# Two groups of block sums on GpSimd instead of VectorE, and another bank for the last token pair's chain

## The chip, the cores and the metric

The kernel runs on one core of one Trainium2 chip. Its time is the device time of one execution in microseconds (us). An execution that was recorded by the hardware profiler has a time of its own, and inside it the span from the first to the last instruction. The engines are TensorE (PE), VectorE (DVE), ScalarE (ACT), GpSimd (POOL) and SyncE (SP, which here only issues DMAs). Each engine works through its own instructions in order; semaphores order the engines against each other.

## The reference

2048 tokens of 512 numbers are normalised (layer norm without weights). The result is the input plus two branches of the normalised tokens `xn`:

```python
qkv = xn @ wqkv                                # 32 heads of 16
logits over the 8 positions s, s-2, ..., s-14  # masked below 0
A = softmax(logits) weighted v, then @ wo
topk_idx = argsort(-(xn @ w_gate))[:, :2]      # 2 of 8 experts
B = sum over the two experts e of gate * (silu(xn @ w1[e]) @ w2[e])   # 512 -> 1792 -> 512
out = x + A + B
```

## The kernel before

**Arithmetic.** Every operand of a matrix product is split into a high and a low part in 16 bits; a product is three passes of PE (high*high, low*high, high*low). `xnT` holds the normalised tokens, transposed, as those two parts.

**Stages on PE, in order.** First the column groups 0 and 1 of `wqkv` for 16 tiles of 128 tokens (`q_pass`, L365 to L383, with the gate's columns in group 0). Then groups 2 and 3 for eight pairs of token tiles (`product`, L481 to L492): a Strassen-like scheme with seven products for each pair `p_`, named m1 to m7, 56 in all. Then 112 blocks of the experts' first product (`up`, L912 to L925) alternating with the second (`down`, L945 to L973), and at the end the product with `wo` (`o_mm`, L1087). The attention itself is computed on DVE beside the experts.

**The sums that the seven products need.** For each group `b` of four token tiles, so for the pairs `2b` and `2b+1`, these steps run before the products m5, m6, m3 and m7 of those pairs:

- `fj_b` (`f_join`, L436): high plus low part of `xnT`, 128x2048, into a 32-bit tile `f`. Groups 0 and 1 (b < NF) use one tile of the pool `fre`; groups 2 and 3 use one of the pool `atp`, which can be opened once `fre` is closed (the task `swapR`).
- `fs_b` (`s_sums`, L444): four sums or differences of 128x512 in that tile.
- `sh_b_0`, `sh_b_1` (`s_hi`, L457): ScalarE copies of 128x1024 to 16 bits, the high part.
- `sl_b_0`, `sl_b_1` (`s_lo`, L462): 128x1024 subtractions, the low part.

All but `sh` are instructions of DVE with two inputs in SBUF.

**The chain of one pair.** The products accumulate in three PSUM banks: a (m1, m6, m7, m4), c (m2) and d (m5, m3). Between the products of bank a ScalarE reads the partial sum out (x11, x12, xu, x21) and between those of d as well (x22); DVE adds parts together (y22, L499; y11 and y12, L507). Bank a is one of two buffers with the tag "up", which the experts' first product uses later. Each pair ends with a store (`pst`).

**Routing.** When the gate's logits of all tokens stand in `glog`, DVE ranks the tokens (`r_top`, L533 to L566: 13 instructions with two SBUF inputs and some with one), PE counts them (`r_count`, L568), DVE goes on (`r_rank`, `r_hot0` to `r_hot2`), PE makes the lists (`r_list1`, `r_list2`, L644), and DVE writes them out (`r_lis`, L647). From then on POOL gathers tokens by indirect DMA (`ga`, L851), SP transposes them (`tx`, L858), and the first block of the experts (`up0`) can start.

**The order.** The order of the instructions on every engine is fixed before the kernel is built, by a planner written out in the file (`Plan.solve`, L72). Each task has an engine, a planned duration, and tasks it depends on (`deps`: their end; `begun`: their begin). PE's tasks have a priority by hand (`prio`), from which their due times follow; from these each other task gets a latest start (`late`), lowered by `HURRY` for `r_lis` and so for what it depends on. Then a list scheduler plays the program through: on each engine the ready task of lowest rank comes next (rank: `prio` on PE, `late` elsewhere). `r_count` and `r_list` have the priority -1000 on PE: they take the next place once they are ready in the plan. The planned durations are `d2(n)` for DVE and `act(n)` for ScalarE, both of n elements in a partition; what engines do to each other's speed is not in it. The order that comes out is final: PE doesn't pass by a task whose input is late.

```python
r = max(r, end[d] + (0.0 if tk[d][0] == t[0] and not tk[d][5] else LAT.get(tk[d][0], 0.08)))
...
c = min((p, r, n) for r, p, n in lst if r <= t0)
```

Of the kernel before, what the change touches and what calls it, by code (L numbers as in the profile page):

```python
# [1 line left out]

# [18 lines left out]
KB = D // P  # L21
# [33 lines left out]

NS = NJ // 2
NP0 = 0
HURRY = dict(r_lis=20.0)
NF = 2
LAT = dict(PE=0.28, ACT=0.16, DVE=0.16, POOL=0.16)  # L60


class Plan:
    def __init__(self):
        self.tasks = {}

    def add(self, name, eng, dur, fn, deps=(), prio=0.0, svc=0.0, early=0.0, begun=(), lead=None, post=0.6):
        assert name not in self.tasks, name
        self.tasks[name] = (eng, dur, fn, [d for d in deps if d is not None], prio, svc, early,
                            [d for d in begun if d is not None], lead, post)  # L70

    def solve(self, start):  # L72
        tk = self.tasks
# [70 lines left out]
                if not left[o]:  # L144
                    release(o)
        assert len(order) == len(tk), [n for n in tk if n not in begin][:20]
        self.begin, self.end, self.order, self.late = begin, end, order, late

    def emit(self, names):
        for n in names:  # L150
# [6 lines left out]

def act(n):
    return 0.18 + n * 0.00087


def mm(*cols):
# [4 lines left out]
def layer_kernel(ctx: ExitStack, tc, x, wqkv, wo, wg, w1, w2, out):  # L167
# [265 lines left out]

    FT, SS = {}, {}

    def f_join(b):  # L436
        f = FT[b] = (fre if b < NF else atp).tile([P, 2048], F32, name=f"f_{b}", tag="f" if b < NF else "og", bufs=1)
        c_ = slice(512 * b, 512 * b + 512)
        v.tensor_tensor(f.rearrange("p (k c) -> p k c", k=KB), xnT[:, 0:KB, c_], xnT[:, KB:2 * KB, c_], op=ALU.add)

    def f_part(b, kh, e_):
        return FT[b].rearrange("p (h k q e t) -> p h k q e t", h=2, k=2, q=2, e=2)[:, kh, :, :, e_, :]

    def s_sums(b):  # L444
        f11, f12, f21, f22 = (f_part(b, kh, e_) for e_ in range(2) for kh in range(2))
        v.tensor_tensor(f22, f21, f22, op=ALU.add)
        v.tensor_tensor(f21, f11, f21, op=ALU.subtract)
        v.tensor_tensor(f11, f22, f11, op=ALU.subtract)
        v.tensor_tensor(f12, f12, f11, op=ALU.subtract)

    def s_dst(b, lo):
        return SS[b][:, lo].rearrange("p (h k m t) -> p k h m t", h=2, k=2, m=4)
# [7 lines left out]
        nc.scalar.copy(s_dst(b, 0)[:, kb], s_src(b)[:, kb])  # L460

    def s_lo(b, kb):  # L462
        v.tensor_tensor(s_dst(b, 1)[:, kb], s_src(b)[:, kb], s_dst(b, 0)[:, kb], op=ALU.subtract)

    s_at = dict(s1=(1, 1), s2=(0, 0), s3=(0, 1), s4=(1, 0))

# [14 lines left out]
    def product(p_, m):  # L481
        bank, l_, r_ = prods[m]
        if (p_, bank) not in MB:
            pp, tg = {"a": (pu, "up"), "c": (py, ("y0", "y2")[p_ % 2]), "d": (py, ("y1", "yt1")[p_ % 2])}[bank]
            MB[p_, bank] = pp.tile([P, 512], F32, name=f"pm_{p_}_{bank}", tag=tg)
        ps = MB[p_, bank][:, 0:384].rearrange("p (c t d) -> p c t d", c=2, t=3)
        t = unit[r_].rearrange("p a (k t c d) -> p a k c t d", k=2, t=3, c=2)
        first, last = m in ("m1", "m2", "m5"), m in ("m2", "m3", "m4")
        for i, (a, b) in enumerate(((0, 0), (1, 0), (0, 1))):
            for k in range(2):  # L490
                nc.tensor.matmul(ps, left_of(p_, l_, a, k), t[:, b, k], start=first and i == 0 and k == 0,  # L491
                                 stop=i == 2 and k == 1, skip_group_check=True)  # L492

    outs_of = dict(x11=("a", 0, 0), y11=("c", 0, 0), x12=("a", 1, 0), x22=("d", 1, 1), xu=("a", 0, 1), x21=("a", 0, 1), y12=("d", 1, 0))

    def take(p_, n):
        if n == "y22":
            e21, e22 = (pair_tile(p_)[:, 2 * cg:2 * cg + 2, :, 1, :] for cg in range(2))
            v.tensor_tensor(e22, e22, e21, op=ALU.add)  # L499
            return  # L500
        bank, cg, e_ = outs_of[n]
        dst = pair_tile(p_)[:, 2 * cg:2 * cg + 2, :, e_, :].rearrange("p c t d -> p (c t) d")
        src = MB[p_, bank][:, 0:384].rearrange("p (n d) -> p n d", d=H2)
        if n[0] == "x":
            nc.scalar.activation(dst, src, AF.Copy, scale=-1.0 / (SW * SX))
        else:
            v.scalar_tensor_tensor(dst, src, -1.0 / (SW * SX), dst, op0=ALU.mult, op1=ALU.add)  # L507
# [669 lines left out]
        add(f"uh_{n}", "ACT", act(768), B(u_hi, n), deps=([n] if n[0] == "t" else after[n]) + old)  # L1177
        add(f"ul_{n}", "DVE", d2(768), B(u_lo, n), deps=[f"uh_{n}"])
    for b in range(NP0 // 2, 4):
        add(f"fj_{b}", "DVE", d2(2048), B(f_join, b), deps=[f"tn_{j}" for j in range(4 * b, 4 * b + 4)] + ([f"sl_{b - 1}_1"] if NP0 // 2 < b != NF else []) + ["swapR"] * (b >= NF))  # L1180
        add(f"fs_{b}", "DVE", 4 * d2(512), B(s_sums, b), deps=[f"fj_{b}"])
        for kb in range(2):
            add(f"sh_{b}_{kb}", "ACT", act(1024), B(s_hi, b, kb), deps=[f"fs_{b}"] + ([f"{m}_{p_}" for p_ in (0, 1) for m in ("m3", "m5", "m6", "m7")] if b == 3 and kb == 0 else []),
                begun=[f"sh_{b}_0" if kb else f"sh_{b - 1}_1" if b > NP0 // 2 else None])
            add(f"sl_{b}_{kb}", "DVE", d2(1024), B(s_lo, b, kb), deps=[f"sh_{b}_{kb}"] + ([f"sl_{b}_0"] if kb else []))
    add("gate", "POOL", 0.6, gate_part, deps=["lgate"], prio=-39.5)
    for i, (cg, j) in enumerate(seq):
        n = 400 if cg == 0 else 384
# [54 lines left out]
    for p_ in range(NP0, NS):  # L1243
        b = p_ // 2
        own = lambda n: f"{n}_{p_}"
        free = {"a": [f"x21_{p_ - 2}"], "c": [f"y11_{p_ - 2}"], "d": [f"y12_{p_ - 2}"]} if p_ > NP0 + 1 else \
            dict(a=ev_of(ups[p_ - NP0 - 2]), c=last_of[(2, 4)[p_ % 2]], d=last_of[(3, 5)[p_ % 2]])
        after = dict(m1=[], m2=[], m6=["x11"], m7=["x12"], m5=[], m4=["xu"], m3=["x22"])
        for i, (m, (bank, l_, r_)) in enumerate(prods.items()):
            ready = [f"sl_{b}_{kb}" for kb in range(2)] if l_[0] == "s" else []  # L1250
            add(own(m), "PE", mm(*[384] * 6), B(product, p_, m), deps=[f"ul_{r_}"] + ready + [own(n) for n in after[m]] +
                (free[bank] if m in ("m1", "m2", "m5") else []), prio=10.0 * len(seq) + 5.0 * (7 * (p_ - NP0) + i))
        keep = [stores[len(order_g) + p_ - 3]]
        for n, m, more in (("x11", "m1", []), ("x22", "m5", []), ("x12", "m6", []), ("y12", "m3", ["x12"]), ("xu", "m7", []),
                           ("y22", "m7", ["xu", "x22"]), ("y11", "m2", ["x11"]), ("x21", "m4", ["y22"])):
            add(own(n), "ACT" if n[0] == "x" else "DVE", act(384) if n[0] == "x" else d2(384), B(take, p_, n),
                deps=[own(m)] + [own(x) for x in more] + keep)
        add(f"pst{p_}", "SP", 0.65, B(p_st, p_), deps=[own(n) for n in ("y11", "y22", "x21", "y12")], svc=2.4)


# [30 lines left out]
    for U in range(NP):  # L1291
# [4 lines left out]
        fr = [f"dn{2 * (U - 3) - 1}_3", f"up{2 * (U - 3) + 1}"] if U > 3 else ([f"up{2 * (U - 3) + 1}"] if U == 3 else [f"{m}_{2 * U + 2 + i}" for i in range(2) for m in ("m3", "m5", "m6", "m7")])  # L1296
        add(f"whi{U}", "ACT", act(n), B(w_hi, U, c_, unit_of(U), unit_of(U - 1)), deps=[f"ld{U}"] + fr, prio=G(2 * U - 3))
        add(f"wlo{U}", "DVE", d2(n), B(w_lo, U, c_), deps=[f"whi{U}"], prio=G(2 * U - 2.5))
    add("silu_t", "ACT", 1.5, lambda: nc.scalar.activation(root, eps, AF.Silu), deps=["x21_7"])
    add("swapL", "X", 0.0, swap_left, begun=stores + ["up0"])  # L1300
    for g, (e, f) in enumerate(blocks):
        U = g // 2
        cap = CAPS[e]
        cols = [cap] * 12 if cap <= 512 else [cap - 64] * 12 + [64] * 12
        bank = [f"si{g - 2}"] if g > 1 else [f"x21_{6 + g}"]
        if g == 0:
            bank += [f"tx0_{t}" for t in range(len(tiles_of(0)))]
        if f == 0 and e:
            bank += [f"tx{e}_{t}" for t in range(len(tiles_of(e)))]
        add(f"up{g}", "PE", mm(*cols), B(up, e, f), deps=bank + [f"wlo{U}"], prio=G(g))  # L1310
        sd = act(cap) + (0.25 if cap > 512 else 0.0)
        hb = [f"dn{g - LAG - 2}_3"] if g >= LAG + 2 else []
        add(f"si{g}", "ACT", sd, B(silu, e, f), deps=[f"up{g}", "swapL"] + ([f"hl{g - 3}"] if g > 2 else []), prio=G(g) - 3)
        add(f"hh{g}", "ACT", act(cap), B(h_hi, e, f), deps=[f"si{g}"] + hb, prio=G(g) - 3)
        add(f"hl{g}", "DVE", d2(cap), B(h_lo, e, f), deps=[f"hh{g}"], prio=G(g))
        t0 = NM if g == NG - 1 else 0
        for t in range(NM + 1):
            cols = [512] * 3 if t < NM else ([2 * (cap - CM)] * 4 + [cap - CM] * 4 if cap - CM <= P else [cap - CM] * 12)
            fr = []
            if f == 0 and e:  # L1320
                fr = [f"ye{e - 1}_{t}"] if t < NM else [f"yt{e - 1}_0", f"yt{e - 1}_1"]
            if g == 0:
                fr += ["y11_6", "y11_7", "y12_6", "y12_7"]
            add(f"dn{g}_{t}", "PE", mm(*cols), B(down, e, f, t), deps=[f"hl{g}", f"wlo{U + 1}"] + fr +
                ([f"dn{g}_{(t - 1) % 4}"] if t != t0 else []), prio=G(g + LAG) + 5 + 0.1 * ((t - t0) % 4))
    ys_use = []
# [223 lines left out]
```

## Time and profile before

| what | us |
|---|---|
| median of 3 runs | 760.68 (760.32 to 761.95) |
| the profiled execution | 759.91 |
| its span | 758.2 |
| PE busy, whole span | 751.8 |
| DVE busy | 665.3 |
| ACT busy | 399.8 |
| POOL busy | 110.1 |
| granted TensorE clock, mean | 1.000 |

"Busy" is the time in which an engine has an instruction under way; for PE the ends are modelled, since matmuls are pipelined. The rest of the page, and views of the same execution by stretches of time, are shown in the prediction where they are used. Positions in time are counted from the start of the span.

### The profile page before, as it was taken

What the parts mean: (1) busy time and instruction counts of PE and PEld (TensorE: products, weight loads), DVE (VectorE), ACT (ScalarE), POOL (GpSimd) and SP (SyncE); (2) the same over time, 40 slices, a digit from 0 to 9 for tenths busy, and PEclk for the clock granted to TensorE, in tenths of its full rate; (3) what the DMA queues carried; (4) which work ended last, traced back from release to release, by engine and by line L of the source; (5) the groups of instructions that cost most, each with busy time, mean ns of one, the idle gap of its engine ahead of it and who ended that gap; (6) DMA issues with size and microseconds to landing.
All of it is one profiled execution on the core that took longest, in us unless ns stands there. A gap on an engine that the chain in (4) does not pass through costs nothing.

```text
span 758.2 us, 12400 instructions
## 1 busy us (share of the span) xinstructions
PE 751.8 (99%) x4917; PEld 413.3 (55%) x4917; DVE 665.3 (88%) x632; ACT 399.8 (53%) x596; POOL 110.1 (15%) x107
## 2 busy tenths in 40 slices
PE   8999999999999999999999999999999999999997
PEld 4555665555555555555555555555555555555544
DVE  7897999999999899989989989999999899737355
ACT  6874356555457445753754574466447554754300
POOL 2010036040001300210030004002100000007171
PEclk9999999999999999999999999999999999999999
DMA  8999889685359647973693599358626943886476
GB/s 278 237 259 314 279 236 309 241 227 167 133 170 224 185 162 210 222 233 117 210 250 140 191 243 261 124 179 206 205 88 170 254 129 111 217 325 208 133 243 203
DMA packets 167377, 157.25 MB, mean 207 GB/s; under 512 B 81505, under 2 KB 135137, under 8 KB 167059
## 3 DMA queue, kind: packets, MB, share of 16 engines
q1 hardware_dynamic: 161571, 139.52, 62.9%
q0 software_dynamic: 5216, 16.88, 7.4%
q8 instruction: 39, 0.64, 0.4%
q14 instruction: 23, 0.19, 0.1%
q10 hardware_dynamic: 528, 0.02, 0.0%
HBM read 108.12 MB, written 29.56 MB: 182 GB/s over the span
## 4 chain that ended last, share of the span: by engine, by line
PE 97%; SPq 1%; DMA 1%; DVE 0%; issue 0%
PE pu L923 13%; PE pu L922 13%; PE pu L924 13%; PE y L955 10%; PE y L954 10%; PE y L953 10%; PE pw L1092 5%; PE pq L383 5%; PE pm_a L491 4%; PE yt L964 3%; PE pq L381 2%; PE pm_d L491 2%; PE yt L965 2%; PE yt L973 2%; PE yt L971 2%; PE yt L972 2%
## 5 line engine op out<-in xcount | busy, mean ns | idle before, releaser
L923 PE MATMUL pu<-xgt,w 128*128 128x64 f16 (+8 forms) x616 | 184.6, 321 | 0.0
L922 PE MATMUL pu<-xgt,w 128*128 128x64 f16 (+8 forms) x616 | 184.4, 321 | 0.0
L924 PE MATMUL pu<-xgt,w 128*128 128x64 f16 (+8 forms) x616 | 180.4, 321 | 0.0
L930 ACT ACTIVATE hs<-pu 128x64 f32<-128x64 f32 (+8 forms) x154 | 69.6, 481 | 186.3 <-PE pu L924 186.1
L897 DVE SCALAR_TENSOR_TENSOR w<-s,w 128x2048 f16<-128x2048 f32 (+1 forms) x57 | 128.2, 2249 | 18.6 <-ACT w L888 18.4
L888 ACT ACTIVATE w<-s 128x2048 f16<-128x2048 f32 (+1 forms) x57 | 107.3, 1883 | 59.2 <-PE yt L965 29.4
L955 PE MATMUL y<-w,hh 128*128 128x512 f16 x336 | 127.5, 379 | 0.0
L954 PE MATMUL y<-w,hh 128*128 128x512 f16 x336 | 127.5, 379 | 0.0
L953 PE MATMUL y<-w,hh 128*128 128x512 f16 x336 | 127.4, 379 | 0.0
L851 POOL DMA_INDIRECT xg<-xr,lis x35 | 64.9, 1854 | 419.1 <-DMA xgt<-xg 359.6
L940 DVE SCALAR_TENSOR_TENSOR hh<-hs,hh 128x550 f16<-128x550 f32 (+7 forms) x112 | 76.6, 687 | 26.2 <-ACT hh L936 26.1
L924 PEld LDWEIGHTS <-w 128*128 128x128 f16 x616 | 58.9, 97 | 48.5
L922 PEld LDWEIGHTS <-w 128*128 128x128 f16 x616 | 59.3, 97 | 41.0
L923 PEld LDWEIGHTS <-w 128*128 128x128 f16 x616 | 59.0, 97 | 40.9
L936 ACT ACTIVATE hh<-hs 128x550 f16<-128x550 f32 (+7 forms) x112 | 70.5, 631 | 3.4
L807 DVE TENSOR_TENSOR pv<-vt,at 128x4096 f32<-128x4096 f32 x16 | 70.7, 4422 | 0.3
L780 DVE TENSOR_TENSOR pq<-kt,qt 128x4096 f32<-128x4096 f32 x16 | 70.7, 4420 | 0.2
L784 DVE TENSOR_REDUCE at<-pq 128x256 f32<-128x4096 f32 x16 | 70.6, 4412 | 0.0
L1075 POOL DMA_INDIRECT yg<-yd,yrow x32 | 36.5, 1139 | 172.5 <-DVE hh L940 146.1
L813 DVE TENSOR_TENSOR pv<-pv 128x2048 f32<-128x2048 f32 (+1 forms) x32 | 56.1, 1753 | 0.2
L955 PEld LDWEIGHTS <-hh 128*128 128x128 f16 x336 | 32.8, 98 | 39.7
L953 PEld LDWEIGHTS <-hh 128*128 128x128 f16 x336 | 32.8, 98 | 34.2
(207 smaller groups left out, 1018.1 us busy)
## 6 DMA issues: line engine op xcount, KB each, us to landing
s<-in_B_w SPq DMA_DIRECT2D x112, 512.0 KB, 4.3
kt<-qd SPq DMA_DIRECT2D x8, 960.0 KB
vt<-qd SPq DMA_DIRECT2D x8, 960.0 KB, 6.5
qd<-qe SPq DMA_DIRECT2D x8, 768.0 KB, 4.5
qd<-qp SPq DMA_DIRECT2D x8, 768.0 KB, 6.7
yd<-ys SPq DMA_DIRECT2D x24, 256.0 KB, 3.1
xr<-xh SPq DMA_DIRECT2D x16, 256.0 KB, 4.2
qt<-qd SPq DMA_DIRECT2D x8, 512.0 KB, 7.0
```

Of the source, the lines that this page charges most:

```text
L780: v.tensor_tensor(A["pr"].rearrange("p (j w d) -> p j w d", w=WIN, d=H2), a_win(A["k", c], hf, False), qb.to_broadcast([P, 8, WIN, H2]), o ...
L784: v.tensor_reduce(A["at", c][:, 8 * hf:8 * hf + 8].rearrange("p j w h -> p (j w h)"), A["pr"].rearrange("p (n d) -> p n d", d=16), axis=AX ...
L807: v.tensor_tensor(A["pr"].rearrange("p (j w h d) -> p j w h d", w=WIN, h=NH, d=16), a_win(A["v", c], hf, True), ab.to_broadcast([P, 8, WIN ...
L888: nc.scalar.activation(w[:, 0, c_], stg[k][:, c_], AF.Copy, scale=SW)
L897: v.scalar_tensor_tensor(w[:, 1, c_], stg[k][:, c_], SW, w[:, 0, c_], op0=ALU.mult, op1=ALU.subtract)
L922: nc.tensor.matmul(ps, a_[:, 0, kb, fs], xh, start=kb == 0, stop=False)
L923: nc.tensor.matmul(ps, a_[:, 0, kb, fs], xl, start=False, stop=False)
L924: nc.tensor.matmul(ps, a_[:, 1, kb, fs], xh, start=False, stop=kb == KB - 1)
L940: v.scalar_tensor_tensor(hh[:, 1, c_], hsd[key, f][:, c_], SH, hh[:, 0, c_], op0=ALU.mult, op1=ALU.subtract)
L953: nc.tensor.matmul(y_, hi, b_[:, 0, :], start=st, stop=False)
L954: nc.tensor.matmul(y_, hi, b_[:, 1, :], start=False, stop=False)
L955: nc.tensor.matmul(y_, lo, b_[:, 0, :], start=False, stop=sp)
```

## The change

`PB = (1, 2)`: `fj`, `fs` and `sl` of the groups 1 and 2 become instructions of GpSimd, with a planned duration of their own, `gp(n)`. For the last pair (`p_ == NS - 1`, so 7) bank a is the bank "yt0" instead of an "up" buffer, free after `r_lis`; the partial result xu goes to the memory of the weight part b11 (`spare`), which m1_7 is the last to read, so that x21 need not wait for y22. `up0` and `up1` wait for the pairs 5 and 6 instead of 6 and 7; the load of ScalarE's table for the experts (`silu_t`) follows x12_7 instead of x21_7. `up0` begins after m4_7 and `up1` after `up0`, as a condition now; `hl0` and `hl1` follow y11_7, y22_7 and y12_7. `HURRY` for `r_lis` is 12 instead of 20. The planner's result is put in order once more, so that a task can be emitted behind others (`behind`) on each engine's unchanged order.

```diff
-HURRY = dict(r_lis=20.0)
+HURRY = dict(r_lis=12.0)
...
+PB = (1, 2)
...
-        self.begin, self.end, self.order, self.late = begin, end, order, late
+        self.begin, self.end, self.late = begin, end, late
...
+            for d in set(tk[n][3]) | set(tk[n][7]) | set(self.behind[n]) | ({prev[e]} if e in prev and e != "X" else set()):
...
+def gp(n):
+    return 0.25 + n * 0.0021
...
+    def s_eng(b):
+        return nc.gpsimd if b in PB else v
...
-        v.tensor_tensor(f.rearrange("p (k c) -> p k c", k=KB), xnT[:, 0:KB, c_], xnT[:, KB:2 * KB, c_], op=ALU.add)
+        s_eng(b).tensor_tensor(f.rearrange("p (k c) -> p k c", k=KB), xnT[:, 0:KB, c_], xnT[:, KB:2 * KB, c_], op=ALU.add)
...
-        v.tensor_tensor(f22, f21, f22, op=ALU.add)
+        s_eng(b).tensor_tensor(f22, f21, f22, op=ALU.add)
...
-        v.tensor_tensor(s_dst(b, 1)[:, kb], s_src(b)[:, kb], s_dst(b, 0)[:, kb], op=ALU.subtract)
+        s_eng(b).tensor_tensor(s_dst(b, 1)[:, kb], s_src(b)[:, kb], s_dst(b, 0)[:, kb], op=ALU.subtract)
...
-            pp, tg = {"a": (pu, "up"), "c": (py, ("y0", "y2")[p_ % 2]), "d": (py, ("y1", "yt1")[p_ % 2])}[bank]
+            pp, tg = {"a": (pu, "up") if p_ < NS - 1 else (py, "yt0"), "c": (py, ("y0", "y2")[p_ % 2]), "d": (py, ("y1", "yt1")[p_ % 2])}[bank]
...
+    def spare():
+        return unit["b11"].rearrange("p a c -> p (a c)").bitcast(F32)[:, 0:384].rearrange("p (n d) -> p n d", d=H2)
...
+            if p_ == NS - 1:
+                e21 = spare()
...
+        if n == "xu" and p_ == NS - 1:
+            dst = spare()
...
+        se, sd = ("POOL", gp) if b in PB else ("DVE", d2)
+        add(f"fj_{b}", se, sd(2048), B(f_join, b), deps=[f"tn_{j}" for j in range(4 * b, 4 * b + 4)] + ([f"sl_{b - 1}_1"] if NP0 // 2 < b != NF else []) + ["swapR"] * (b >= NF))
+        add(f"fs_{b}", se, 4 * sd(512), B(s_sums, b), deps=[f"fj_{b}"])
...
+            add(f"sl_{b}_{kb}", se, sd(1024), B(s_lo, b, kb), deps=[f"sh_{b}_{kb}"] + ([f"sl_{b}_0"] if kb else []))
...
+        if p_ == NS - 1:
+            free["a"] = ["r_lis"]
...
-                           ("y22", "m7", ["xu", "x22"]), ("y11", "m2", ["x11"]), ("x21", "m4", ["y22"])):
+                           ("y22", "m7", ["xu", "x22"]), ("y11", "m2", ["x11"]), ("x21", "m4", ["y22"] if p_ < NS - 1 else [])):
...
-    add("silu_t", "ACT", 1.5, lambda: nc.scalar.activation(root, eps, AF.Silu), deps=["x21_7"])
-    add("swapL", "X", 0.0, swap_left, begun=stores + ["up0"])
+    add("silu_t", "ACT", 1.5, lambda: nc.scalar.activation(root, eps, AF.Silu), deps=["x12_7"])
+    add("swapL", "X", 0.0, swap_left, begun=["up0", f"x21_{NS - 1}"], behind=stores)
...
-        bank = [f"si{g - 2}"] if g > 1 else [f"x21_{6 + g}"]
+        bank = [f"si{g - 2}"] if g > 1 else [f"x21_{NS - 3 + g}"]
...
-                fr += ["y11_6", "y11_7", "y12_6", "y12_7"]
+                fr += ["y11_6", "y11_7", "y12_6", "y12_7", "x21_7"]
```

More of the change, by code (lines that the diff above doesn't have):

```diff
@@ L1 @@
+import heapq
 from contextlib import ExitStack
@@ L64, in __init__, with add @@
     def __init__(self):
-        self.tasks = {}
-    def add(self, name, eng, dur, fn, deps=(), prio=0.0, svc=0.0, early=0.0, begun=(), lead=None, post=0.6):
+        self.tasks, self.behind = {}, {}
+    def add(self, name, eng, dur, fn, deps=(), prio=0.0, svc=0.0, early=0.0, begun=(), lead=None, post=0.6, behind=()):
         assert name not in self.tasks, name
@@ L70, in add @@
                             [d for d in begun if d is not None], lead, post)
+        self.behind[name] = list(behind)
     def solve(self, start):
@@ L146, in solve @@
         assert len(order) == len(tk), [n for n in tk if n not in begin][:20]
-        self.begin, self.end, self.order, self.late = begin, end, order, late
+        self.begin, self.end, self.late = begin, end, late
+        need, outs, prev = {n: 0 for n in tk}, {n: [] for n in tk}, {}
+        rank = {n: i for i, n in enumerate(order)}
+        for n in order:
+            e = tk[n][0]
+            for d in set(tk[n][3]) | set(tk[n][7]) | set(self.behind[n]) | ({prev[e]} if e in prev and e != "X" else set()):
+                outs[d].append(n)
+                need[n] += 1
+            prev[e] = n
+        heap = [rank[n] for n in tk if not need[n]]
+        heapq.heapify(heap)
+        self.order = []
+        while heap:
+            n = order[heapq.heappop(heap)]
+            self.order.append(n)
+            for o in outs[n]:
+                need[o] -= 1
+                if not need[o]:
+                    heapq.heappush(heap, rank[o])
+        assert len(self.order) == len(tk)
     def emit(self, names):
@@ L445, in s_sums @@
         f11, f12, f21, f22 = (f_part(b, kh, e_) for e_ in range(2) for kh in range(2))
[L446 to L449, printed above, removed]
+        s_eng(b).tensor_tensor(f22, f21, f22, op=ALU.add)
+        s_eng(b).tensor_tensor(f21, f11, f21, op=ALU.subtract)
+        s_eng(b).tensor_tensor(f11, f22, f11, op=ALU.subtract)
+        s_eng(b).tensor_tensor(f12, f12, f11, op=ALU.subtract)
     def s_dst(b, lo):
@@ L494, in layer_kernel @@
     outs_of = dict(x11=("a", 0, 0), y11=("c", 0, 0), x12=("a", 1, 0), x22=("d", 1, 1), xu=("a", 0, 1), x21=("a", 0, 1), y12=("d", 1, 0))
+    def spare():
+        return unit["b11"].rearrange("p a c -> p (a c)").bitcast(F32)[:, 0:384].rearrange("p (n d) -> p n d", d=H2)
     def take(p_, n):
         if n == "y22":
-            e21, e22 = (pair_tile(p_)[:, 2 * cg:2 * cg + 2, :, 1, :] for cg in range(2))
+            e21, e22 = (pair_tile(p_)[:, 2 * cg:2 * cg + 2, :, 1, :].rearrange("p c t d -> p (c t) d") for cg in range(2))
+            if p_ == NS - 1:
+                e21 = spare()
             v.tensor_tensor(e22, e22, e21, op=ALU.add)
@@ L1179, in layer_kernel @@
     for b in range(NP0 // 2, 4):
-        add(f"fj_{b}", "DVE", d2(2048), B(f_join, b), deps=[f"tn_{j}" for j in range(4 * b, 4 * b + 4)] + ([f"sl_{b - 1}_1"] if NP0 // 2 < b != NF else []) + ["swapR"] * (b >= NF))
-        add(f"fs_{b}", "DVE", 4 * d2(512), B(s_sums, b), deps=[f"fj_{b}"])
+        se, sd = ("POOL", gp) if b in PB else ("DVE", d2)
+        add(f"fj_{b}", se, sd(2048), B(f_join, b), deps=[f"tn_{j}" for j in range(4 * b, 4 * b + 4)] + ([f"sl_{b - 1}_1"] if NP0 // 2 < b != NF else []) + ["swapR"] * (b >= NF))
+        add(f"fs_{b}", se, 4 * sd(512), B(s_sums, b), deps=[f"fj_{b}"])
         for kb in range(2):
@@ L1184, in layer_kernel @@
                 begun=[f"sh_{b}_0" if kb else f"sh_{b - 1}_1" if b > NP0 // 2 else None])
-            add(f"sl_{b}_{kb}", "DVE", d2(1024), B(s_lo, b, kb), deps=[f"sh_{b}_{kb}"] + ([f"sl_{b}_0"] if kb else []))
+            add(f"sl_{b}_{kb}", se, sd(1024), B(s_lo, b, kb), deps=[f"sh_{b}_{kb}"] + ([f"sl_{b}_0"] if kb else []))
     add("gate", "POOL", 0.6, gate_part, deps=["lgate"], prio=-39.5)
@@ L1254, in layer_kernel @@
         for n, m, more in (("x11", "m1", []), ("x22", "m5", []), ("x12", "m6", []), ("y12", "m3", ["x12"]), ("xu", "m7", []),
-                           ("y22", "m7", ["xu", "x22"]), ("y11", "m2", ["x11"]), ("x21", "m4", ["y22"])):
+                           ("y22", "m7", ["xu", "x22"]), ("y11", "m2", ["x11"]), ("x21", "m4", ["y22"] if p_ < NS - 1 else [])):
             add(own(n), "ACT" if n[0] == "x" else "DVE", act(384) if n[0] == "x" else d2(384), B(take, p_, n),
-                deps=[own(m)] + [own(x) for x in more] + keep)
+                deps=[own(m)] + [own(x) for x in more] + keep + (["m1_7"] if n == "xu" and p_ == NS - 1 else []))
         add(f"pst{p_}", "SP", 0.65, B(p_st, p_), deps=[own(n) for n in ("y11", "y22", "x21", "y12")], svc=2.4)
@@ L1309, in layer_kernel @@
             bank += [f"tx{e}_{t}" for t in range(len(tiles_of(e)))]
-        add(f"up{g}", "PE", mm(*cols), B(up, e, f), deps=bank + [f"wlo{U}"], prio=G(g))
+        add(f"up{g}", "PE", mm(*cols), B(up, e, f), deps=bank + [f"wlo{U}"], prio=G(g), begun=[] if g > 1 else [f"up{g - 1}" if g else f"m4_{NS - 1}"])
         sd = act(cap) + (0.25 if cap > 512 else 0.0)
@@ L1314, in layer_kernel @@
         add(f"hh{g}", "ACT", act(cap), B(h_hi, e, f), deps=[f"si{g}"] + hb, prio=G(g) - 3)
-        add(f"hl{g}", "DVE", d2(cap), B(h_lo, e, f), deps=[f"hh{g}"], prio=G(g))
+        add(f"hl{g}", "DVE", d2(cap), B(h_lo, e, f), deps=[f"hh{g}"], prio=G(g),
+            begun=[] if g > 1 else [f"{n}_{NS - 1}" for n in ("y11", "y22", "y12")])
         t0 = NM if g == NG - 1 else 0
```

## The prediction

> **What bounds the kernel now.** The page comes first: how long the span is, which engine is full, which engine the chain of work that ended last runs through.
>
> ```profile
> span 758.2 us, 12400 instructions
> ...
> PE 751.8 (99%) x4917; PEld 413.3 (55%) x4917; DVE 665.3 (88%) x632; ACT 399.8 (53%) x596; POOL 110.1 (15%) x107
> ...
> PE 97%; SPq 1%; DMA 1%; DVE 0%; issue 0%
> ```
>
> PE is busy for 751.8 of 758.2 us and holds 97% of the chain. DVE's 88% is a large number off that chain. Second, all waits of PE in the span, and the last of them in PE's timeline:
>
> ```profile
> PE pwarm L254 <- DVE eps L208: 1.3, 1, 1.3
> PE pt L351 <- DVE rs L324: 0.3, 1, 0.3
> PE pt L351 <- DVE xn L327: 0.2, 1, 0.2
> ```
>
> ```profile
> 17.06 0.63 PE L351 MATMUL pt<-ident,xn 128*128 128x128 f32 x4 [0.33 <-DVE rs L324]
> ```
>
> PE waits 1.8 us in all, and the last wait ends at 17.06. Third, the stages that the change works in, and what follows them:
>
> ```profile
> core 0: us, PE busy (x) PEld busy (x) DVE busy (x) ACT busy (x) POOL busy (x), PEclk, DMA share, GB/s
> ...
> 50.30:66.00 15.70, 15.70 (x97) 9.28 (x95) 11.86 (x13) 8.38 (x21) 0.00 (x0) 1.00 1.07 291
> 66.00:73.20 7.20, 7.20 (x48) 4.35 (x46) 6.53 (x23) 2.89 (x5) 0.00 (x0) 1.00 1.04 369
> 73.20:101.40 28.20, 28.20 (x203) 17.27 (x201) 27.09 (x51) 13.39 (x25) 2.31 (x3) 1.00 0.75 246
> ...
> 128.64:712.30 583.66, 583.66 (x3922) 318.64 (x3920) 529.72 (x397) 319.18 (x430) 69.99 (x43) 1.00 0.66 193
> ```
>
> In each stretch the first two numbers are equal: PE is never idle, at the full clock (1.00). The change takes no matmul away. So **DVE time that is saved here has no PE wait to shorten**; the change can only leave PE as full as it is, or open gaps. Any gap after 17.06 is added to the time at its full length, because all later PE work is behind it. The question is thus where PE, whose order is fixed, waits for DVE or POOL. Fourth, those places in the chain:
>
> ```profile
> 72.53 0.65 PE pq L381 x4
> 73.18 0.01 PE pr L570
> 73.19 0.03 PE pr L571
> 73.22 0.99 PE pm_a L491 x6
> ...
> 90.78 0.40 PE pl L644 x16
> ...
> 127.67 0.97 PE pm_a L491 x6
> 128.64 0.20 PE pu L922
> ```
>
> r_count (L570) stands in the middle of PE's queue at 73.18, all 56 products behind it; r_list1 stands at 90.78. DVE's side of it:
>
> ```profile
> 49.08 1.22 DVE L463 TENSOR_TENSOR sw<-f,sw 128x1024 f16<-128x1024 f32 x1 [0.71 <-ACT sw L460]
> ...
> 55.45 0.95 DVE L418 TENSOR_TENSOR wqs<-wqs,wqs 128x768 f32<-128x768 f32 x1
> ...
> 66.02 0.29 DVE L535 TENSOR_TENSOR lg<-glog 128x128 f32<-128x128 f32 x1 [3.26 <-ACT glog L406]
> ...
> 71.87 0.17 DVE L566 CAST rsum<-sc_a 128x8 f16<-128x8 f32 x1
> ...
> 88.83 2.29 DVE L439 TENSOR_TENSOR f<-xnT 128x2048 f32<-128x2048 f16 x1
> ...
> 97.42 0.19 DVE L647 CAST lis<-pl 128x40 int32<-128x40 f32 x1
> ```
>
> r_top runs from 66.02 to 71.87 + 0.17 = 72.04, and PE takes r_count at 73.18: **a margin of 1.14 us**. r_top can't begin sooner, since it follows the last logits from ScalarE, after 3.26 us of idle DVE.
>
> **The change part by part.** What leaves DVE, by groups of lines (the four of `s_sums` lie between the two shown):
>
> ```profile
> L463 DVE TENSOR_TENSOR sw<-f,sw 128x1024 f16<-128x1024 f32 x8 | 9.5, 1214 | 1.2 <-ACT sw L460 1.2
> L439 DVE TENSOR_TENSOR f<-xnT 128x2048 f32<-128x2048 f16 x4 | 9.1, 2282 | 0.1
> L448 DVE TENSOR_TENSOR f<-f 128x512 f32<-128x512 f32 x4 | 2.8, 693 | 0.1
> L446 DVE TENSOR_TENSOR f<-f 128x512 f32<-128x512 f32 x4 | 2.7, 679 | 0.0
> ```
>
> One group of sums costs DVE 2.28 + 4 x 0.69 + 2 x 1.21 = 7.46 us, two groups 14.9 us. Group 1 lay ahead of the 3.26 us of idle time; group 2 lay beside r_hot and r_lis (fj_2 at 88.83). For PE both are worth 0, as above. A DVE that is ahead starts the attention sooner, which ends off the chain: also 0.
>
> What POOL pays the trace doesn't show at this size. From below, DVE's own 7.46 us for a group. From above, POOL's largest instruction that reads SBUF, the L233 shown next: from the end of the DVE instruction that it seems to stand behind (42.00 + 1.16 = 43.16) to its own end (42.16 + 2.54 = 44.70) it takes 1.54 us for 512 elements, so 3.0 ns for each of the 6144 of a group: 18.5 us. I take the planned durations in the diff, `gp`, which lie between: fj 4.55, fs 4 x 1.33 = 5.3, each sl 2.40, together 14.65 us. [...]
>
> Now the part that decides: **do the two engines run beside each other?** The only long POOL instruction of before that reads SBUF beside DVE, and one POOL wait that goes the other way:
>
> ```profile
> 42.16 2.54 POOL L233 TENSOR_SCALAR_AFFINE_SELECT mask<-mask 128x512 f32<-128x512 f32 x1 [36.49 <-DVE mask L1132]
> ```
>
> ```profile
> 42.00 1.16 DVE L463 TENSOR_TENSOR sw<-f,sw 128x1024 f16<-128x1024 f32 x1
> 43.08 2.00 DVE L339 SCALAR_TENSOR_TENSOR xh<-xn,rs,xh 128x512 f16<-128x512 f32 x1
> ```
>
> ```profile
> L339 DVE SCALAR_TENSOR_TENSOR xh<-xn,rs,xh x12: 720/746/2005, 18.5 to 47.6; 128x512 f16<-128x512 f32 x12
> ```
>
> ```profile
> 116.52 4.75 POOL L851 DMA_INDIRECT xg<-xr,lis  x1 [0.30 <-issue]
> ```
>
> ```profile
> 116.03 4.42 DVE L780 TENSOR_TENSOR pq<-kt,qt 128x4096 f32<-128x4096 f32 x1
> 120.36 2.29 DVE L897 SCALAR_TENSOR_TENSOR w<-s,w 128x2048 f16<-128x2048 f32 x1
> ```
>
> L339 has twelve executions with a median of 746 ns; the one under POOL's L233 took 2005 ns, 1.26 more, and ended 0.38 us after L233 did. It has two inputs in SBUF, as have `fj`, `fs`, `sl` and most of r_top. The other way round, POOL's gather at 116.52 ended only 0.82 us after the DVE instruction with two inputs that it had run into, while the next such DVE instruction was under way. I read this as the two engines taking turns, one instruction each. [...]
>
> So the sum, by turns. sl_0_1 ends at 49.08 + 1.22 = 50.30 and frees `f`, so fj_1 starts then. Alone, group 1 takes 4.55 + 5.3, a ScalarE copy between (1.05, the row below), and 4.8: to 66.0. Four of DVE's weight instructions (0.95 each, L418 and L432, from 55.45 on) take turns with it: to 69.8. At 66.0, when r_top may begin, POOL has before it the rest of group 1, 3.8, then fj_2 4.55 and fs_2 5.3: 13.65 us. r_top has 13 instructions with two inputs, enough to meet every one of these seven or so POOL instructions, so it pays 13.65, less 1.5 for its reductions, copy and memsets that need no turn. With the margin of 1.14 us taken off, PE waits at r_count for 13.65 - 1.5 - 1.14 = **11.0 us**. sl_2, 4.8 us more, falls under r_rank, whose lateness the next stop (r_list1) sees; I count 0, as the planned DVE queue between has fj_2 and fs_2 (5.0 us) taken out and other work to shift, with 4.8 as the other bound. fj_2 may also have to wait until the tiles under it are stored; then it meets r_rank instead of r_top, and the price moves to r_list1.
>
> ```profile
> 48.00 1.05 ACT L460 CAST sw<-f 128x1024 f16<-128x1024 f32 x1
> ```
>
> The bank of the last pair: x21_7 without y22_7, the table load sooner, up0 free of pair 6. In the chain above up0 follows m4_7 without a gap (127.67 + 0.97 = 128.64), so there is nothing to gain; m1_7 waits for r_lis, which is over at 97.61, against products that run until 128.64: 0 while r_lis is less than about 20 us late. HURRY lets r_lis come up to 8 us later in the plan. Behind it stand five gathers and transposes on POOL's and SP's queues:
>
> ```profile
> 114.88 2.78 SPq L858 DMA_TRANSPOSE xgt<-xg  x1
> ```
>
> ```profile
> DMA to landing us min/median/max: 5.7/6.3/6.9
> ```
>
> The last of them has landed by 114.88 + 6.9 = 121.8, 6.8 us before up0. Within that, 0.
>
> Sum against the profiled execution: 759.91 + 11.0 = 770.9. The median of the runs shown is 760.68, 0.77 above it: **771.7 us**.
>
> **The rivals.**
>
> [...]
>
> [...]
>
> *Faster.* Needs PE idle time to remove. After 17.06 there is none on record, and no task before that is touched.
>
> *Slower by more.* With POOL at 18.5 us a group, or sl_2 paid too, the waits grow to 11.0 + 4.8 = 15.8 or more: 776 to 779.
>
> **How the numbers follow.** Forecast (turns, PE held at r_count and r_list, 762 to 777): 0.57. Hidden: 0.36. Elsewhere: 0.04. Faster: 0.03. A measurement of this kernel can tell about 0.2%, 1.5 us, from no change. So slower 0.61, same 0.36, faster 0.03. The forecast's own range is 764 to 777; to leave out no more than 2 in 10, the range must reach down to the hidden case: 760.0 to 777.0.
>
> **What would show it.** Right: PE waits for DVE's L566 (PE's r_count) for about 11 us near 73 to 84; r_top's instructions with two inputs take 1 to 5 us each in place of 0.29, ending with POOL's `f` instructions one by one; fj_1 on POOL lasts about 4.55 from about 50.3; no new wait after up0. Wrong: PE without a gap from 66 to 101, r_top still 6 us long beside a busy POOL. [...]

## The result and the profile after

| | median, us | ratio to before |
|---|---|---|
| before, same chip | 760.78 (760.32 to 761.95) | 1 |
| changed | 768.55 (767.98 to 769.88) | 1.0102, 95% interval 1.0084 to 1.0121 |

The changed kernel is 7.8 us slower. Its profiled execution took 768.02 us, with a span of 766.2. The line numbers below are those of the changed kernel (r_top begins at L571 instead of L535; `f_join`, `s_sums` and `s_lo` are L468, L475 to L478 and L492).

All waits of PE in the changed kernel:

```profile
PE pr L606 <- DVE rsum L602: 5.8, 1, 5.8
PE pwarm L280 <- DVE eps L234: 1.3, 1, 1.3
PE pq L409 <- DMA xnT<-xh: 0.2, 1, 0.2
PE pt L377 <- DVE xn L353: 0.2, 1, 0.2
```

One line is new: r_count waits 5.8 us for the last result of r_top. The stages (PE's busy time and the granted clock, PEclk, are the columns to read):

```profile
50.30:66.00 15.70, 15.70 (x96) 9.29 (x95) 11.81 (x7) 8.58 (x21) 14.23 (x7) 1.00 1.06 295
66.00:72.80 6.80, 6.80 (x44) 4.11 (x42) 6.56 (x6) 2.70 (x5) 6.64 (x4) 1.00 1.04 369
72.80:82.30 9.50, 3.73 (x16) 1.74 (x14) 9.05 (x21) 1.71 (x3) 2.54 (x3) 0.64 0.83 292
82.30:136.00 53.70, 53.70 (x359) 32.63 (x358) 50.45 (x67) 27.95 (x48) 18.35 (x12) 1.00 0.81 241
```

In these stretches PE is full everywhere but between 72.8 and 82.3, and there the clock was 0.64 on average. In finer pieces, it was halved from a point within PE's wait until PE had worked again for 3.4 us:

```profile
73.00:75.20 2.20, 0.00 (x0) 0.00 (x0) 2.13 (x3) 1.22 (x2) 2.12 (x2) 1.00 0.21 80
75.40:82.00 6.60, 3.23 (x13) 1.54 (x13) 6.26 (x17) 0.49 (x1) 0.10 (x1) 0.50 1.02 354
82.20:84.00 1.80, 1.80 (x12) 1.08 (x11) 1.63 (x10) 0.88 (x2) 0.00 (x0) 1.00 1.00 422
```

The chain of work shows what that cost: six matmuls of a product took 0.97 us before.

```profile
78.93 0.03 PE pr L607
78.96 1.94 PE pm_a L520 x6
80.90 1.66 PE pm_d L520 x6
82.55 1.46 PE pm_a L520 x9
```

The first two products after the wait took 1.94 and 1.66 us, (1.94 - 0.97) + (1.66 - 0.97) = 1.7 us too much. The wait and the slow products make 5.8 + 1.7 = 7.5 of the 8.0 us by which the profiled span grew (758.2 to 766.2). `up0`, behind all products, begins at 136.01 in place of 128.64, 7.4 us later; the other 0.6 us arise behind it and are not explained. Now GpSimd and VectorE beside each other in that stretch:

```profile
61.45 4.61 POOL L492 TENSOR_TENSOR sw<-f,sw 128x1024 f16<-128x1024 f32 x2 [1.16 <-ACT sw L489]
66.02 4.12 POOL L468 TENSOR_TENSOR f<-xnT 128x2048 f32<-128x2048 f16 x1
70.21 1.26 POOL L475 TENSOR_TENSOR f<-f 128x512 f32<-128x512 f32 x1
71.55 1.26 POOL L476 TENSOR_TENSOR f<-f 128x512 f32<-128x512 f32 x1
72.89 1.26 POOL L477 TENSOR_TENSOR f<-f 128x512 f32<-128x512 f32 x1
74.24 1.26 POOL L478 TENSOR_TENSOR f<-f 128x512 f32<-128x512 f32 x1
```

```profile
66.24 0.29 DVE L575 TENSOR_REDUCE m<-lg 128x16 f32<-128x128 f32 x1
66.56 3.72 DVE L577 TENSOR_TENSOR eq<-lg,m 128x128 f32<-128x128 f32 x1
70.39 1.24 DVE L578 TENSOR_TENSOR eq<-eq,rev_e 128x128 f32<-128x128 f32 x1
71.66 0.29 DVE L580 TENSOR_REDUCE im<-eq 128x16 f32<-128x128 f32 x1
71.98 0.98 DVE L582 TENSOR_TENSOR hot<-eq,im 128x128 f32<-128x128 f32 x1
73.00 1.31 DVE L587 SCALAR_TENSOR_TENSOR l<-hot,lg 128x128 f32<-128x128 f32 x1
74.34 0.29 DVE L575 TENSOR_REDUCE m<-l 128x16 f32<-128x128 f32 x1
74.66 0.99 DVE L577 TENSOR_TENSOR eq<-l,m 128x128 f32<-128x128 f32 x1
75.68 0.29 DVE L578 TENSOR_TENSOR eq<-eq,rev_e 128x128 f32<-128x128 f32 x1
...
78.54 0.17 DVE L602 CAST rsum<-sc_a 128x8 f16<-128x8 f32 x1
```

Before, the instructions shown took 0.29 us each, and the last one 0.17. The same comparison as the one of 3.72 us, in the kernel before:

```profile
66.67 0.29 DVE L541 TENSOR_TENSOR eq<-lg,m 128x128 f32<-128x128 f32 x1
```

The five with two inputs that met a GpSimd instruction took 3.72, 1.24, 0.98, 1.31 and 0.99: each waited for one, first for fj_2 and then for the four of fs_2, and then had its turn. The reductions, with one input, stayed at 0.29 beside the same GpSimd instructions. When GpSimd was done, at 75.5, the next instruction took 0.29 again. r_top, 6.0 us before, lasted from 65.83 to 78.71: 12.9 us.

### The profile page after: what moved, and what is told of

The parts are those of the page before. It is cut to its first block, busy times and chain, and to the rows that moved or that the text cites. A ratio compares the mean times of both kernels' runs of the same rounds, so it can differ in the third digit from the quotient of the medians.

```text
span 766.2 us, 12395 instructions
## 1 busy us (share of the span) xinstructions
PE 753.7 (98%) x4917; PEld 414.4 (54%) x4917; DVE 666.1 (87%) x618; ACT 399.6 (52%) x596; POOL 132.6 (17%) x121
## 4 chain that ended last, share of the span: by engine, by line
PE 94%; DVE 3%; DMA 1%; ACT 1%; issue 0%; ACTq 0%; DVEq 0%
PE pu L960 13%; PE pu L958 13%; PE pu L959 13%; PE y L991 9%; PE y L990 9%; PE y L989 9%; PE pw L1128 5%; PE pm_a L520 4%; PE yt L1000 3%; PE pq L409 3%; PE pm_d L520 2%; PE yt L1001 2%; PE yt L1007 2%; PE yt L1009 2%; PE yt L1008 2%; PE pq L407 1%
## 5 line engine op out<-in xcount | busy, mean ns | idle before, releaser
L887 POOL DMA_INDIRECT xg<-xr,lis x35 | 58.5, 1672 | 378.4 <-DMA xgt<-xg 362.3
```

## The experiments

The theory: GpSimd's reading instructions and VectorE's instructions with two inputs in SBUF exclude each other by turns, so r_top is late, and PE's fixed order waits for it. The rivals: the new order, bank or HURRY; the sums on GpSimd as such; any work on GpSimd.

**All sums back on VectorE, the rest of the change kept.**

```diff
-PB = (1, 2)
+PB = ()
```

> The changed kernel with PB empty: all four groups of sums back on VectorE, everything else of the change kept (bank of the last pair, HURRY 12, the new conditions). Theory of turns (VectorE's instructions with two SBUF inputs and GpSimd's reading instructions exclude each other, so r_top is stretched and PE waits at r_count): r_top lasts 6.0 us again, PE does not wait at r_count, 760.8 us, ratio to before 0.998 to 1.002. Rival, the new order or bank is what costs: PE still waits, 767 to 769. Second rival, HURRY lets r_lis come so late that up0 waits for its gathered tokens: 1 to 3 us, 762 to 764.

Measured: 761.56 us, ratio 1.0013 (1.0003 to 1.0022). r_top lasted 6.0 us and r_count didn't wait, so GpSimd's part makes nearly all of the loss. The small rest has a row of its own in PE's waits:

```profile
PE pm_a L520 <- ACT wx_b L541: 0.6, 1, 0.6
```

This is m4_7 waiting at about 128 for xu to be read out to the spare memory (wx_b), so here the new bank's chain costs 0.6 us. A second row, 1.0 us at 45 for a DMA (xnT<-xh), lies long before r_top; it is 0 to 1.0 us in the runs, whatever the edit. up0 didn't wait for its tokens: the HURRY rival falls.

**GpSimd's part alone, on the kernel before.** The edit is that of `PB`, `gp`, `s_eng` and the three planned tasks in the diff above, and nothing else.

> The kernel before with nothing but the sums of groups 1 and 2 on GpSimd (with their planned durations); bank, HURRY 20 and conditions as before. Theory of turns: r_top lasts 12 to 13 us, PE waits about 6 us at r_count and runs slow for about 3 us after, 768.5 us, ratio 1.008 to 1.012. Rival, order or bank: 760.8, ratio 1.000.

Measured: 770.19 us, ratio 1.0126 (1.0109 to 1.0143).

```profile
PE pr L578 <- DVE rsum L574: 5.7, 1, 5.7
...
PE pu L930 <- ACT qp L513: 0.6, 1, 0.6
```

The wait at r_count is the same with the old bank and HURRY; the ratio is a little above the expected 1.008 to 1.012. The second line is a wait of up0 for the last pairs' old bank; the changed kernel hasn't got it. In this pair of profiles the bank saves beside GpSimd's sums about what it costs without them; that the 0.6 us carry through to the time is not shown.

**Only one group on GpSimd.**

```diff
-PB = (1, 2)
+PB = (1,)
```

> The changed kernel with PB = (1,): only group 1 on GpSimd. Theory of turns: group 1 ends on GpSimd at about 66, as r_top begins, so r_top meets at most the end of it: r_top 6 to 6.5 us, wait at r_count below 0.3 us, 760.8 to 761.5 us. If any GpSimd sums at all were the cause (their price, the tiles, the semaphores): half of the loss or more, 764 to 768.

> The changed kernel with PB = (2,): only group 2 on GpSimd. Theory of turns: group 2 lies beside r_top; if fj_2 starts at 66 as in the changed kernel, 768; if GpSimd, now free before, starts it some us sooner, r_top meets less of it: wait at r_count 2 to 5 us, 763 to 767. If the price of group 1 were what counts: 760.8.

Measured: 761.19 us with group 1, ratio 1.0008 (0.9998 to 1.0017), and no wait at r_count: the same amount of sums on GpSimd costs no time there, as GpSimd has ended at 66.4, where r_top begins (its first instruction took 0.44 us, the others 0.29 again). VectorE pays even so: between 49 and 61.5, beside group 1, one weight part takes 4.71 us and four take 1.9 to 2.0 in place of 0.95, and its busy time is 665.4 us against 665.3 before, with 7.5 us of sums fewer. It had room for that, 3.3 us of idle time before r_top in the kernel before. The 0.6 us row of m4_7 stands here too. With group 2 (`PB = (2,)`): 766.63 us, 1.0080 (1.0063 to 1.0097), by another way than I had expected. GpSimd, free before, began fj_2 at 48.81 and met group 1 on VectorE, here its `fs_1`:

```profile
58.44 1.59 POOL L477 TENSOR_TENSOR f<-f 128x512 f32<-128x512 f32 x1
```

```profile
58.94 1.64 DVE L476 TENSOR_TENSOR f<-f 128x512 f32<-128x512 f32 x1
60.62 1.64 DVE L477 TENSOR_TENSOR f<-f 128x512 f32<-128x512 f32 x1
...
69.64 0.28 DVE L571 TENSOR_TENSOR lg<-glog 128x128 f32<-128x128 f32 x1
```

Here the sums take 1.64 us in place of 0.69, and r_top, itself undisturbed, begins 3.6 us late. PE waits at four places, 1.5, 1.0, 2.2 and 0.5 us; the first of them is for ScalarE, which had stood still for 7.25 us until `fs_1`'s last sum. So it isn't the meeting with r_top as such that costs, but VectorE's time in turns, wherever PE's order next asks for VectorE.

**Only GpSimd work beside r_top, without moving any sum.** On the kernel before:

```diff
+    def beside(reads, n):
+        g_ = glog[:, 8:NJ, :].rearrange("p j e -> p (j e)")
+        nc.gpsimd.tensor_tensor(scr, g_, g_, op=ALU.add)
+        m_ = mask.rearrange("p j w h -> p (j w h)")
+        for _ in range(n):
+            if reads:
+                nc.gpsimd.tensor_tensor(m_, m_, m_, op=ALU.add)
+            else:
+                nc.gpsimd.memset(scr, 0.0)
...
+    add("beside", "POOL", 9.0, B(beside, True, 8), deps=gl + ["c_mask"])
```

> The kernel before, sums all on VectorE, with extra work on GpSimd from the last logits on: one addition of 128 elements and eight of 512 that read SBUF with both inputs (the mask doubled in place; it holds 0 and -1e9, so the result stays). No task depends on them until much later. Theory of turns: each meets one of r_top's 13 instructions with two inputs, as fs_2 did (0.7 to 1.0 us each): r_top 12 to 13 us, PE waits 5 to 6 us at r_count and runs slow after, 767 to 769, ratio 1.008 to 1.011. Rival, the loss comes from dependencies or the order of the sums themselves: 760.6.

> As the run with reading GpSimd additions, but 48 memsets of 128 elements instead of the eight additions: GpSimd is busy as long (5 us or more) beside r_top, writing SBUF and not reading it. Theory of turns for reading instructions only: r_top 6.0 to 6.5 us, no wait at r_count, 760.6, ratio 0.999 to 1.002. Rival, any GpSimd work beside VectorE stretches it: r_top 9 us or more, 764 to 768.

Measured: with the reading additions 766.77 us, ratio 1.0081 (1.0065 to 1.0098); with the memsets (`B(beside, False, 48)`) 760.59 us, 0.9998 (0.9988 to 1.0007). The additions:

```profile
66.79 8.86 POOL L1269 TENSOR_TENSOR mask<-mask 128x512 f32<-128x512 f32 x8
```

```profile
68.08 1.01 DVE L542 TENSOR_TENSOR eq<-eq,rev_e 128x128 f32<-128x128 f32 x1
```

```profile
PE pr L570 <- DVE rsum L566: 4.2, 1, 4.2
```

And the memsets, with VectorE in the middle of them:

```profile
67.04 12.51 POOL L1271 MEMSET scr<- 128x128 f32 x48
```

```profile
67.08 0.29 DVE L541 TENSOR_TENSOR eq<-lg,m 128x128 f32<-128x128 f32 x1
67.47 0.29 DVE L542 TENSOR_TENSOR eq<-eq,rev_e 128x128 f32<-128x128 f32 x1
```

8.9 us of reading work on which nothing depends stretch r_top and bring the wait back; 12.5 us of writing work leave r_top's instructions with two inputs at 0.29 or less, and r_top at 6.1 us. This is the sharpest of the tests: neither the order nor the dependencies differ between the two. The memsets are also shorter than the additions, 12.51 / 48 = 0.26 us against 8.86 / 8 = 1.11, but a turn of 0.26 us would show beside 0.29. My expected sizes for the additions were a little high: r_top ended at 77.57, 11.3 us after it began, eight of its instructions having met the eight additions, and PE waited 4.2 us, not 5 to 6.

**Group 2 held back until r_top is over**, in two runs. First by a condition in the plan:

```diff
-        add(f"fj_{b}", se, sd(2048), B(f_join, b), deps=[f"tn_{j}" for j in range(4 * b, 4 * b + 4)] + ([f"sl_{b - 1}_1"] if NP0 // 2 < b != NF else []) + ["swapR"] * (b >= NF))
+        add(f"fj_{b}", se, sd(2048), B(f_join, b), deps=[f"tn_{j}" for j in range(4 * b, 4 * b + 4)] + ([f"sl_{b - 1}_1"] if NP0 // 2 < b != NF else []) + ["swapR"] * (b >= NF) + ["r_top"] * (b == 2))
```

> The changed kernel with one more condition: fj_2 on GpSimd begins after r_top. Theory of turns: r_top lasts 6.0 us and PE does not wait at r_count, but now r_rank (15 instructions with two inputs) takes turns with fj_2 and fs_2 and is 5 to 7 us late, so PE waits at r_list1 or at a product behind it: 3 to 6 us in all, 763 to 767. Rival, only the meeting with r_top costs: no wait, 760.8.

Measured: 770.38 us, ratio 1.0131 (1.0114 to 1.0148), a miss: a condition of the planner orders the plan and makes no semaphore, and since fj_2 reads nothing of r_top's, GpSimd began it at 66.56, as r_top's second instruction was about to start. So r_top met fj_2 as in the changed kernel, and the run does not test what it was made for. Then by the data:

```diff
+        if b == 2:
+            nc.gpsimd.tensor_copy(seen, R["rsum"])
```

> The changed kernel with fj_2 on GpSimd held back by the data: GpSimd first copies eight numbers of rsum, r_top's last result (the condition of the run before held in the plan alone). Theory of turns: r_top 6.0 us, no wait at r_count; fj_2 now meets ul_t2 and the next VectorE instructions, fs_2 the following ones: m6_0 waits 1 to 2 us for ul_t2, r_rank begins 5 to 7 us late, m4_0 and r_list1 wait, 3 to 7 us in all: 763 to 768. Rival, only the meeting with r_top costs: 760.8 to 762.

Measured: 772.69 us, ratio 1.0154 (1.0137 to 1.0171). r_top lasted 6 us and r_count had no wait, but:

```profile
73.81 4.77 POOL L471 TENSOR_TENSOR f<-xnT 128x2048 f32<-128x2048 f16 x1
```

```profile
74.88 4.51 DVE L458 SCALAR_TENSOR_TENSOR wq<-wqs,wq 128x768 f16<-128x768 f32 x1 [0.22 <-ACT wq L455]
```

```profile
PE pm_a L523 <- DVE wq L458: 5.6, 1, 5.6
PE pm_a L523 <- ACT qp L544: 2.7, 1, 2.7
```

The weight part after r_top (ul_t2) now takes 4.51 us in place of 0.96, and another part of the weights behind it 1.91. ScalarE, which works in order, stood 3.85 us for that one with a readout of bank a behind it; for this readout PE waited 2.7 us, at 80. fs_2 and then sl_2 met r_rank, which lasted from 81.3 to 93.0, 11.8 us in place of the changed kernel's 5.6. The 5.6 us, at 88, are for the weight part that VectorE does after r_rank. The loss moved to later stops and grew beyond the 3 to 7 us that I had expected, since sl_2 met r_rank too, and since PE's clock was halved for 6.9 us with the second wait (mean granted clock 0.996).

**r_count later on PE.**

```diff
-    add("r_count", "PE", 0.15, r_count, deps=["r_top"], prio=-1000)
+    add("r_count", "PE", 0.15, r_count, deps=["r_top"], prio=-1000, begun=["m5_1"])
```

> The changed kernel with r_count on PE only after m5_1 has begun (eight products later in the plan). Theory, it is VectorE's lateness that PE meets, wherever the next stop stands: r_top still 12.9 us, no wait at r_count; PE does three products (2.9 us) and then waits for the weight part ul_t2, which VectorE forms after r_top, 3 to 4 us, and 0 to 3 us more at later stops: 764 to 768. Rival, only the place of r_count is at fault: 760.8 to 762.

Measured: 768.82 us, ratio 1.0102 (1.0086 to 1.0119), 0.8 us above the expected range. r_count no longer waits; two products do (a third, m4_7, waits 0.6 us for wx_b as above):

```profile
PE pm_a L520 <- DVE wq L458: 3.1, 1, 3.1
PE pm_a L520 <- ACT qp L541: 2.0, 1, 2.0
```

The rival that only the place of r_count is at fault falls. The later r_count has a price of its own: r_rank is later too and meets sl_2 (two of its instructions take 2.10 and 2.05 us).

**PE kept busy through the wait.** The results of the added matmuls are not used.

```diff
+        pk = py.tile([P, D], F32, name="pk", tag="misc")
+        for _ in range(24):
+            nc.tensor.matmul(pk, xnT[:, 0, 0:P], xnT[:, 0, 0:D], start=True, stop=True)
```

> The changed kernel with 24 extra matmuls of 512 columns (5.2 us) ahead of r_count on PE, in the time in which PE waited; their result is not used. Theory, PE runs slow after it has waited: the wait at r_count shrinks to about 0.7 us, the products after it take 162 ns each from the first on instead of 320 ns, and 1.6 us of the changed kernel's 7.8 us loss go: 766.9 us, ratio to before 1.007 to 1.009. Rival, the slow products have another cause (their data, VectorE or GpSimd beside them): they stay at 320 ns, 768.5 us, ratio 1.010.

Measured: 769.56 us, ratio 1.0126 (1.0109 to 1.0143). The wait at r_count fell to 0.5 us and the products after it ran at full speed, so idle PE time is what made them slow:

```profile
79.43 0.99 PE pm_a L520 x6
80.42 0.97 PE pm_d L520 x6
```

But the expected 1.6 us weren't gained: PE, now ahead, waited 2.2 us for the weight part ul_t4 and 0.5 at r_list1. With the products ahead, ScalarE's copies let sl_2 begin at 87.81, while r_rank was still under way, and two of its last instructions took 2.1 us each in place of 0.2. In the changed kernel sl_2 began at 88.97, after that. So removing the slow products gained nothing in this run, because VectorE's lateness took it at the next stops; what they would be worth with the meeting of sl_2 and r_rank unchanged is not shown.

**Group 1 on GpSimd with the old bank and HURRY** (the part alone, with `PB = (1,)`).

> The kernel before with group 1 alone on GpSimd; bank, HURRY 20 and conditions as before. Theory of turns: as with the other conditions, group 1 is over as r_top begins: no wait at r_count, 760.5 to 761.0, ratio 0.999 to 1.001. The 0.7 us wait of m4_7 for xu in the two runs without GpSimd's group 2 is from the change of bank and is absent here.

Measured: 760.83 us, ratio 0.9999 (0.9989 to 1.0008), without PE waits between 46 and 700. It is the best place found for a group on GpSimd, and it gains nothing: PE had no wait to lose, and VectorE's busy time (666.0 us) isn't shorter either.

## Why the prediction was right

**PE can't gain: right.** No run was faster than before by more than its interval, and the runs with group 1 on GpSimd are level. They hardly test what a VectorE with less to do is worth, though, since its busy time didn't fall: 665.4 and 666.0 us there and 666.1 in the changed kernel, against 665.3 before.

**Turns: right.** The row of L339 that the prediction read as a turn is now five rows in one stretch, and the pair of runs with reading and writing GpSimd work shows the turns without the change: r_top took 11.3 us beside the reading additions (`d1_pool_reads`), and its instructions with two inputs 0.29 us or less each beside the memsets (`d2_pool_writes`).

**The place, r_count: right.** The new wait is L602 to L606, as written.

**The size: the forecast was 11.0 us on the profiled execution, measured 8.1 (768.02 against 759.91).** These terms differ.

- "The rest of group 1, 3.8": measured 0. The prediction let fj_1 start at 50.30, where sl_0_1 ended before. In the new order sl_0_1 comes sooner (46.70), fj_1 began at 48.01, and group 1 was over at 66.06. The earlier start is 2.3 us of the 3.8; the rest is that the group took 18.05 us and not the 69.8 - 50.3 = 19.5 of the forecast, above all `fs_1`, 7.7 us with its four turns in place of 5.3 + 3.8.
- "fj_2 4.55 and fs_2 5.3": r_top paid 3.72 - 0.29 = 3.4 for fj_2, since its first such instruction came 0.54 us after fj_2's start, and 0.95 + 0.69 + 1.02 + 0.70 = 3.4 for fs_2, whose instructions are shorter than planned (1.26 us with a turn of 0.29 in it, so 1.0 alone, against 1.33). Together 6.8; the forecast had 9.85 less 1.5 for the reductions, copy and memsets, so 8.35. That those need no turn was my estimate. Beside reading GpSimd instructions three reductions took 0.29 us in the changed kernel and two memsets 0.11 in the run with the additions, as without GpSimd; r_top's copy met none, so for it no run shows this.
- Not in the sum: PE's slow products after the wait, 1.7 us, and the 0.6 us behind up0 that are not explained.

With the margin at r_count, 1.14 in the prediction and 72.83 - (65.83 + 6.02) = 1.0 here (the last four matmuls before r_count begin at 72.18 and take 0.65 us): 6.8 - 1.0 = 5.8, the wait in the profile. That the total came within 3 us is partly luck: the first two terms were too large and the third was missing.

**sl_2 at 0: the number is right, the reason is not.** The prediction put it under r_rank. It began at 88.97, 13.5 us after GpSimd had ended fs_2, because its ScalarE copies stood behind the readouts of the late products, and r_rank was over at 87.8. The run with PE kept busy shows that the 4.8 us were rightly kept as a bound.

**Bank and HURRY at 0: nearly.** Waits of 0.6 us stand on either side: with the new bank at m4_7 in the runs without group 2 on GpSimd and in the one with r_count later, with the old bank at up0 in the run of GpSimd's part alone. Which it is depends on the order.

## What to carry to other kernels

Moving two-input work from VectorE to GpSimd shared out no time in these runs while VectorE had two-input work too: each waited for the other (up to 3.72 us in place of 0.29 in r_top; on GpSimd a sum of 128x512 took 1.86 to 1.87 us beside the weight parts and 1.26 beside r_top's shorter instructions), and fj was about twice as long on GpSimd (4.50 and 4.12 us, turns included, against 2.28). What a stretch in which VectorE is idle or does work with one input would give was not shown: no run here has such a one. Group 1 was free for another reason: it stretched VectorE's weight parts, but it ended as r_top began, and PE waited for none of them. And by the argument above, which no run here tests, moved work gains only if the engine that bounds the kernel was waiting for VectorE. A planner whose durations don't know of such turns puts the consumers, here PE's r_count, where VectorE's late result must be met with a wait (5.8 us).

## What the runs showed that was not expected

**PE runs at half speed after its longer waits.** After the 5.8 us wait the matmuls of 384 columns followed each other at about 320 ns in place of 162 for 3.4 us, with the granted clock at 0.50. The run with reading additions shows it after a wait of 4.2 us, there for 5.5 us of work, the run with r_count later after one of 3.1, and the run with fj_2 behind rsum after one of 5.6. The 2.7 us wait of that last run and the waits of up to 2.2 us with group 2 alone were followed by none. The mean granted clock of the profiled execution is 0.996 with the additions, 0.997 with r_count later and 0.996 with fj_2 behind rsum, against 1.000 before and with group 2 alone. The clock was halved for 6.8 us in the changed kernel (75.3 to 82.15), for 6.8 with the additions, 6.9 with fj_2 behind rsum and 3.4 with r_count later. It fell 2.3 us after PE's last matmul had ended (73.0 in the profile) in the changed kernel, and 2.7 to 3.2 us after in the other three. What sets these lengths is not shown.

**A copy with one input can be held too; one row shows it.** In the run with PE kept busy, a conversion from 32 to 16 bits took 2.10 us beside sl_2, in place of 0.17:

```profile
90.00 2.10 DVE L654 CAST tok<-tokf 128x16 f16<-128x16 f32 x1
```

**Whether a planned condition is a real one** is seen in the trace alone: the run with fj_2 "after r_top" had GpSimd at it at 66.56, 0.2 us after r_top began (66.40).
